# A convolution and low-rank mixer kernel: the batch quarters load in another order, the last quarter of batch 2 waits behind a GpSimd copy and a convolution, and one table is made by a multiplication

## The chip, the cores and the metric

The kernel runs on one core of a Trainium2 chip. The metric is the device time of one execution in microseconds (us); shorter is better. Engines are called PE (TensorE matmul), PEld (its weight load), DVE (VectorE), ACT (ScalarE), POOL (GpSimd) and SP (SyncE); L12 is line 12 of the kernel.

## The reference

The input `x` has 8 batches of 4224 rows by 192 columns. First comes a causal convolution of 7 taps along the rows, with one softmaxed set of weights for each of 8 groups of 24 columns. Then comes a mixer: a low-rank product along the rows, a residual, and a two-layer network along the columns.

```python
w = np.exp(weight - weight.max(-1)); w = w / (w.sum(-1) + 1e-9)       # 8 heads, 7 taps
x_unf = x_pad[:, idx, :].reshape(B, S, K, H, group)
y = np.einsum('hk,bskhg->bshg', w, x_unf).reshape(B, S, D)             # the convolution
h = y.transpose(0, 2, 1) @ U @ V                                       # rank 32, along the rows
u = y + h.transpose(0, 2, 1)
out = u + np.maximum(u @ w_ch1, 0.0) @ w_ch2                           # 192 -> 768 -> 192
```

## The kernel before, in words

All 8 x 33 = 264 tiles of 128 rows are numbered in one row and cut into 33 groups of 8 tiles. A group `g` goes through these steps: `h_group(g)` (L499) multiplies the low-rank factor by `V` on PE (L467) and DVE adds the convolution's result (L490), which gives `u_sb`; `transp(g)` (L507) has SP issue a DMA transpose of `u_sb` into `uT` (L509); `w1(g)` (L573) is the first layer on PE (36 matmuls, L585), whose results ACT (L599) and DVE (L601) take through the ReLU into `rl_sb`; `w2(g)` (L606) is the second layer (L612), DVE adds the residual (L621), and SP issues the store (L629). The stores and the transposes stand in one queue, SP's, in program order. PSUM has 8 banks, which all matmul results use in turn (`bank()`, L56).

A batch `b` is loaded by `x_part` (L76, L79) in four DMAs, cast from float32 to bfloat16, that POOL issues. The tile `x_sb` has two halves of 64 partitions (`r` = 0 and 1), and each half is cut in two along the columns of blocks; the list `XP` (L84) gives the order of these quarters. Two `x_sb` buffers serve in turn, and `x_load` (L639) holds a quarter back until a given matmul is done (`held`, L631).

Batches 0 and 1 are convolved by `conv` (L363), which needs the loaded tile alone. Batches from 2 on use `conv32` (L329), which also needs a copy `xb_sb`, shifted by one block of rows. `x_shift` (L294) makes it in six steps on POOL: `same(s0, s1)` (L301) copies all 128 partitions of some blocks, and `ahead(r, s0, s1)` (L313) overwrites a quarter of the partitions of one half. There is one `xb_sb` buffer.

The order of everything is written by hand in `SLOTS` (L648): each slot names the groups for `w1`, the groups for `w2`, and the jobs that stand between the quarters of `w2`. `do` (L785) carries out a job: "h4" is `h_group(4)` with its transpose, "l2:3" loads quarter 3 of batch 2, "d1" is the convolution of batch 1 by `conv`, followed by `transp(3)`, which is held until the last matmul of that convolution; "x2:6" runs six steps of `x_shift(2)`; "c2:0:3:AAD" is a part of `conv32` for batch 2; "t1" and "s1" are the low-rank sum of batch 1. From batch 3 on, the quarters are loaded from inside `w1` (`LOADS`, L699), and with each load one of the remaining `x_shift` steps is issued.

At the head, `rq` (L153 to L156) is a table of 128 rows by 2 columns: 32 and -128 times the row's quarter number. L178 and L229 read it on the way to the convolution's bands.

Of the kernel before, what the change touches and what calls it, by code (L numbers as in the profile page):

```python
# [7 lines left out]
ALU = mybir.AluOpType  # L8
# [6 lines left out]
def kernel(  # L15
# [10 lines left out]
    nc = tc.nc  # L26
# [14 lines left out]
    QB = 32  # L41
# [14 lines left out]
    def bank():  # L56
        return psp.tile([P, 512], F32, name="ps", tag="ps")
# [9 lines left out]
    NB0 = 32  # L67
    NB1 = S // HB - NB0
# [4 lines left out]
    def x_zero(b, eng):  # L73
        eng.memzero(xt[b][0:HB, 0, :])

    def x_part(b, r, s0, s1):  # L76

        blk = NB0 * r + s0 - 1
        return nc.gpsimd.dma_start(  # L79
            out=xt[b][HB * r : HB * r + HB, s0:s1, :],  # L80
            in_=x[b, blk * HB : (blk + s1 - s0) * HB, :].rearrange("(j p) d -> p j d", p=HB),
        )

    XP = [(0, 1, 17), (0, 17, NB0 + 1), (1, 0, 18), (1, 18, NB1 + 1)]  # L84

    KP = [{0: (0, 10), 1: (0, 10)}, {1: (10, NB1 // 2)}, {0: (10, NB0 // 2)}]

# [15 lines left out]
    def iota(t, pattern, base, mul):  # L103
# [20 lines left out]
        out=Ur[:, 0:nfull, :], in_=U4[0 : nfull * P, :].rearrange("(k p) c -> p k c", p=P)  # L124
# [10 lines left out]
    for q in range(4):  # L135
        src = moe_V[:, 0 : full * 8 * P].rearrange("r (k q t) -> r k q t", q=4, t=2 * P)
        nc.gpsimd.dma_start(
            out=V_sb[32 * q : 32 * q + 32, 0 : 2 * full, :].rearrange(
                "r (k a) t -> r k (a t)", a=2
            ),  # L140
# [3 lines left out]
    for hf in range(2):  # L144
        nc.gpsimd.dma_start(
            out=W1_sb[HB * hf : HB * hf + HB, :, :],
# [5 lines left out]

    rq = cst.tile([P, 2], F32, name="rq")  # L153
    for r in range(4):
        for n, v in enumerate((32.0, -128.0)):
            nc.vector.memset(rq[QB * r : QB * r + QB, n : n + 1], v * r)  # L156
    wps = bank()

    def idle(n, w=4):
# [15 lines left out]
    for hh in range(2):  # L175
# [3 lines left out]
        out=dif[:], in0=dif[:], scalar1=rq[:, 0:1], scalar2=None, op0=ALU.add  # L179
# [5 lines left out]
        out=d_sb[:],  # L185
        in0=w_sb[:],
# [7 lines left out]
        out=hot[:],  # L194
        in0=dif[:].unsqueeze(1).to_broadcast([P, KC, BW]),
# [5 lines left out]
        out=ident[:], in0=fp[:], scalar1=float(P), scalar2=None, op0=ALU.is_equal  # L201
# [9 lines left out]
        out=c_sb[:].rearrange("p k h -> p h k"),  # L211
        in0=e_sb[:],
# [4 lines left out]
    for hh in range(2):  # L217
# [3 lines left out]
            out=pr[:],  # L221
            in0=hot[:].unsqueeze(2).to_broadcast([P, KC, HQ, BW]),
# [7 lines left out]
        out=Eq[:], in0=efp[:], scalar1=rq[:, 1:2], scalar2=None, op0=ALU.is_equal  # L230
# [3 lines left out]
        out=fp[:], in0=fp[:], scalar1=R - 1, scalar2=None, op0=ALU.bitwise_and  # L234
# [3 lines left out]
        out=R4[:], in0=fp[:], scalar1=0.0, scalar2=None, op0=ALU.is_equal  # L238
# [55 lines left out]
    def x_shift(b):  # L294


        xbt[b] = xbs.tile([P, NB1, D], BF16, name="xb_sb")

        def same(s0, s1, *rest):
            def step():  # L300
                nc.gpsimd.tensor_copy(out=xbt[b][:, s0:s1, :], in_=xt[b][:, s0 + 1 : s1 + 1, :])  # L301
                for t0, t1 in rest:
                    nc.gpsimd.tensor_copy(
                        out=xbt[b][HB : HB + QB, t0:t1, :],
                        in_=xt[b][HB : HB + QB, t0 + 1 : t1 + 1, :],
                    )

            return step

        def ahead(r, s0, s1):  # L310
            def step():
                q = slice(HB * r + QB, HB * r + HB)
                nc.gpsimd.tensor_copy(out=xbt[b][q, s0:s1, :], in_=xt[b][q, s0:s1, :])  # L313

            return step

        m = NB0 // 2
        return [
            same(0, m),
            same(m, NB0, (NB0, NB1)),  # L320
            ahead(0, 0, m),
            ahead(0, m, NB0),
            ahead(1, 0, m),
            ahead(1, m, NB1),
        ]

    steps = []

    def conv32(b, h0, nh, engs):  # L329


        if yt[b] is None:
            yt[b] = ys.tile([P, NT, D], BF16, name="y_sb")
        nk = (NB0 // 2, NB1 // 2)
        for n in range(nh):
            h = h0 + n
            hs = slice(h * GS, h * GS + GS)
            pp = [bank(), bank()]
            for cg in range(4):
                t, w, st = (  # L340
                    (xt[b], bands[h // HQ][:, h % HQ, QB : 2 * QB], 1 + cg // 2)
                    if cg % 2
                    else (xbt[b], band2[:, h, :], cg // 2)
                )
                for r in range(2):
                    hr = slice(HB * r, HB * r + HB)
                    nc.tensor.matmul(  # L347
                        out=pp[r][QB * cg : QB * cg + QB, 0 : nk[r] * GS],
                        lhsT=w[hr],
                        rhs=t[hr, st : st + 2 * nk[r] - 1 : 2, hs],  # L350
                        start=True,
                        stop=True,
                        tile_position=(HB * r, QB * cg),
                    )
            for part in range(2):
                j0 = NB0 // 2 * part
                evac(
                    engs[(2 * n + part) % len(engs)],
                    yt[b][:, j0 : j0 + nk[part], hs],
                    pp[part][:, 0 : nk[part] * GS].rearrange("p (k a) -> p k a", a=GS),  # L360
                )
# [58 lines left out]
    def tt_split(b, p):  # L420

        hi = sml.tile([P, D], BF16, name="tt_hi")
        lo = sml.tile([P, D], BF16, name="tt_lo")
        nc.scalar.activation(out=hi[:], in_=p[:, 0:D], func=ACT.Copy)  # L424
        nc.vector.tensor_tensor(out=lo[:], in0=p[:, 0:D], in1=hi[:], op=ALU.subtract)
        ttb[b] += [hi, lo]
# [6 lines left out]
    def tt_sum(b):  # L433
        p = bank()
        for n, part in enumerate(ttb[b]):
            nc.tensor.matmul(  # L436
                out=p[:, 0:D],
                lhsT=R4[:],
                rhs=part[:],
                start=(n == 0),  # L440
                stop=(n + 1 == len(ttb[b])),
            )
        tt_done(b, p)
# [10 lines left out]
    done = []  # L454
# [44 lines left out]
    def h_group(g):  # L499
        t0, t1 = g * GT, g * GT + GT  # L500
        while t0 < t1:
            b = t0 // NT
            te = min(t1, (b + 1) * NT)
            h_tiles(b, t0 - b * NT, te - b * NT)
            t0 = te

    def transp(g):  # L507
        uTt[g] = uts.tile([P, 4, 3, P], BF16, name="uT")
        return nc.sync.dma_start_transpose(  # L509
            out=uTt[g][:].rearrange("p i c t -> p (i c) t"),  # L510
            in_=ut[g][:].rearrange("p i c f k -> p (i c f k)"),
        )
# [118 lines left out]
    def held(ins, after):  # L631
        tc.add_manual_dep(
            ins.ins,
            after.ins.name,
            mybir.DependencyInfo(mybir.DependencyClass.Sync, mybir.DependencyReason.DATA),
            reason="transfer held back",
        )

    def x_load(b, q, after):  # L639
        if q == 0:  # L640
            x_tile(b)
            x_zero(b, nc.gpsimd)
        held(x_part(b, *XP[q]), after)

# [2 lines left out]

    SLOTS = [  # L648
        ([0], [], {}),
        ([1], [0], {0: ["h0", "l2:0", "l2:1"], 1: ["h3", "l2:2"], 2: ["l2:3"]}),  # L650
        ([2], [1], {0: ["d1", "h1"], 1: ["t1"], 3: ["s1"], 4: ["h4", "x2:6"]}),
        ([3], [2], {1: ["h5"], 3: ["h6"]}),
        (
            [4, 5],
# [14 lines left out]
    for k in range(5, 14):  # L669
# [13 lines left out]
        elif k < 10:  # L683
            b = k - 2
# [40 lines left out]
    x_zero(1, nc.gpsimd)  # L725
    x_part(1, *XP[0])
    o = 0
    for r, (k0, k1) in KP[2].items():
        j = NB0 // 2 * r + k0
        nc.gpsimd.tensor_copy(  # L730
            out=U4_sb[:, o : o + k1 - k0, :, :],
# [9 lines left out]
        out=V_sb[0:32, 2 * (NT // 8), :], in_=moe_V[:, (NT - 1) * P : NT * P]  # L741
# [32 lines left out]
    band2 = cst.tile([P, H, QB], BF16, name="band2")  # L774
    for xp in XP[1:]:
        x_part(1, *xp)
    for r in range(4):
        q = slice(QB * r, QB * r + QB)
        for hh in range(2):
            nc.gpsimd.tensor_copy(  # L780
                out=band2[q, HQ * hh : HQ * hh + HQ, :],
# [3 lines left out]
    def do(what):  # L785
        if what[0] == "c":
            b, h0, n, engs = what[1:].split(":")
            conv32(int(b), int(h0), int(n), engs)
            return
        if what[0] == "d":  # L790
            for h in range(H):
                last = conv(int(what[1:]), h, 1, [0, 1], "AA" if h == 2 else "AD")
            held(transp(3), last)
            return
        if what[0] == "l":
            b, q = (int(v) for v in what[1:].split(":"))
            x_load(b, q, done[-1])
            return
        if what[0] == "x":
            b, n = (int(v) for v in what[1:].split(":"))  # L800
            steps.extend(x_shift(b))
            for _ in range(n):
                steps.pop(0)()
            return
        n = int(what[1:])
        if what[0] == "h":
            h_group(n)
            if n > 1 and n != 3:
                transp(n)
        elif what[0] == "t":  # L810
            tt_split(n, tt_mm(n, range(NT)))
        else:
            tt_sum(n)
# [55 lines left out]
```

## Time and profile before

| | us |
|---|---|
| median of 3 runs (lowest, highest) | 325.52 (325.27, 325.65) |
| the profiled execution's own time | 325.04 |
| span of the profiled execution | 323.3 |
| PE busy in the span | 316.1 (98%) |
| DVE busy | 268.7 (83%) |
| ACT busy | 169.6 (52%) |
| POOL busy | 141.1 (44%) |

The span is counted from the first instruction to the last end; 325.04 - 323.3 = 1.7 us lie around it. A matmul's end is modelled in the profile, so that a busy PE is not PE at its peak. In the views a wait is written "who waited <- what released it".

### The profile page before, as it was taken

What the parts mean: (1) busy time and instruction counts of PE and PEld (TensorE: products, weight loads), DVE (VectorE), ACT (ScalarE), POOL (GpSimd) and SP (SyncE); (2) the same over time, 40 slices, a digit from 0 to 9 for tenths busy, and PEclk for the clock granted to TensorE, in tenths of its full rate; (3) what the DMA queues carried; (4) which work ended last, traced back from release to release, by engine and by line L of the source; (5) the groups of instructions that cost most, each with busy time, mean ns of one, the idle gap of its engine ahead of it and who ended that gap; (6) DMA issues with size and microseconds to landing.
All of it is one profiled execution on the core that took longest, in us unless ns stands there. A gap on an engine that the chain in (4) does not pass through costs nothing.

```text
span 323.3 us, 9598 instructions
## 1 busy us (share of the span) xinstructions
PE 316.1 (98%) x4004; PEld 223.7 (69%) x4004; DVE 268.7 (83%) x553; ACT 169.6 (52%) x344; POOL 141.1 (44%) x108
## 2 busy tenths in 40 slices
PE   7999999999999999999999999999999999999994
PEld 3757577578678648877864884696796497497494
DVE  6779989987977986997898699789888888896853
ACT  1766723960973496098249509915804903903900
POOL 8764069828947984991986596000000000000000
PEclk9999999999999999999999999999999999999999
DMA  9999994999999999899589965148098089059044
GB/s 105 192 194 171 193 237 102 189 172 273 210 123 199 255 140 193 155 178 214 163 213 183 209 162 159 52 132 241 23 190 250 3 165 276 2 143 248 2 133 162
DMA packets 122443, 53.39 MB, mean 165 GB/s; under 512 B 87712, under 2 KB 122400, under 8 KB 122400
## 3 DMA queue, kind: packets, MB, share of 16 engines
q1 hardware_dynamic: 84528, 38.08, 47.4%
q0 software_dynamic: 37728, 14.60, 39.2%
q8 instruction: 31, 0.51, 0.6%
q14 instruction: 12, 0.10, 0.1%
q10 hardware_dynamic: 144, 0.10, 0.1%
HBM read 29.22 MB, written 25.95 MB: 171 GB/s over the span
## 4 chain that ended last, share of the span: by engine, by line
PE 90%; ACT 4%; DMA 2%; DVE 2%; issue 1%; POOL 0%; POOLq 0%
PE ps L612 42%; PE ps L585 39%; PE ps L347 3%; PE ps L467 3%; DMA x_sb<-in_x_dram 2%; PE ps L410 2%; ACT rl_sb L599 2%; ACT y_sb L264 2%; PE ps L377 1%; DVE u_sb L490 1%; DVE rl_sb L601 1%; PE ps L436 0%; PE ps L532 0%; POOL x_sb L79 0%; DVE out_sb L621 0%
## 5 line engine op out<-in xcount | busy, mean ns | idle before, releaser
L599 ACT ACTIVATE rl_sb<-ps 128x512 bf16<-128x512 f32 x233 | 124.3, 604 | 107.7 <-PE ps L585 100.1
L612 PE MATMUL ps<-W_sb,rl_sb 128*128 128x192 bf16 x1584 | 141.2, 246 | 0.2
L612 PEld LDWEIGHTS <-rl_sb 128*128 128x128 bf16 x1584 | 128.3, 98 | 11.8 <-issue 11.4
L585 PE MATMUL ps<-uT,W_sb 64*128 64x512 bf16 x1188 | 131.5, 376 | 0.4 <-DVE uT L266 0.2
L601 DVE TENSOR_SCALAR rl_sb<-ps 128x512 bf16<-128x512 f32 x163 | 105.2, 686 | 15.0 <-PE ps L585 14.7
L585 PEld LDWEIGHTS <-W_sb 64*128 64x128 bf16 x1188 | 67.2, 94 | 60.2 <-issue 3.6
L621 DVE TENSOR_TENSOR out_sb<-ps,u_sb 128x384 f32<-128x384 f32 (+1 forms) x133 | 70.2, 548 | 25.5 <-PE ps L612 25.1
L313 POOL COPY xb_sb<-x_sb 32x3072 bf16<-32x3072 bf16 (+1 forms) x24 | 67.4, 2824 | 0.5
L490 DVE TENSOR_TENSOR u_sb<-y_sb,ps 128x192 bf16<-128x192 bf16 (+1 forms) x168 | 66.2, 458 | 0.0
L301 POOL COPY xb_sb<-x_sb 128x3072 bf16<-128x3072 bf16 x12 | 32.6, 2742 | 43.0 <-PE ps L347 31.3
L264 ACT ACTIVATE y_sb<-ps 128x384 bf16<-128x384 f32 (+4 forms) x90 | 38.3, 520 | 9.7 <-PE ps L347 7.4
L79 POOL DMA_DIRECT2D x_sb<-in_x_dram x32 | 27.1, 853 | 11.4 <-PE ps L467 7.7
L266 DVE CAST y_sb<-ps 128x408 bf16<-128x408 f32 (+4 forms) x36 | 19.1, 577 | 1.3 <-PE ps L377 1.2
L467 PE MATMUL ps<-tt_sb,V_sb 32*128 32x192 bf16 x264 | 12.4, 246 | 0.1
L347 PE MATMUL ps<-xb_sb,band 64*32 64x384 bf16 x192 | 12.1, 332 | 0.0
L347 PE MATMUL ps<-x_sb,band 64*32 64x384 bf16 x192 | 12.1, 333 | 0.0
L467 PEld LDWEIGHTS <-V_sb 32*128 32x128 bf16 x264 | 4.7, 92 | 7.3 <-issue 7.3
L424 ACT ACTIVATE tt_hi<-ps 128x192 bf16<-128x192 f32 x8 | 2.6, 330 | 11.9 <-PE ps L410 11.9
L377 PE MATMUL ps<-x_sb,band 64*64 64x240 bf16 (+3 forms) x192 | 7.9, 276 | 0.4 <-DMA x_sb<-in_x_dram 0.3
L347 PEld LDWEIGHTS <-band 64*32 64x32 bf16 x384 | 4.6, 89 | 5.2 <-issue 2.4
L377 PEld LDWEIGHTS <-band 64*64 64x64 bf16 x192 | 6.0, 106 | 2.2 <-issue 1.5
L161 PE MATMUL ps<-zz 128*128 128x512 f32 (+1 forms) x10 | 6.4, 785 | 1.1 <-DVE zz L151 1.1
(64 smaller groups left out, 68.0 us busy)
## 6 DMA issues: line engine op xcount, KB each, us to landing
out_dram<-out_sb SPq DMA_DIRECT2D x131, 192.0 KB, 2.9
x_sb<-in_x_dram POOLq DMA_DIRECT2D x14, 384.0 KB, 7.4
x_sb<-in_x_dram POOLq DMA_DIRECT2D x7, 432.0 KB, 7.6
x_sb<-in_x_dram POOLq DMA_DIRECT2D x7, 408.0 KB, 8.9
W_sb<-in_moe_w_ch_dram POOLq DMA_DIRECT2D x3, 288.0 KB, 7.6
x_sb<-in_x_dram POOLq DMA_DIRECT2D x1, 504.0 KB, 7.4
uT<-u_sb SPq DMA_TRANSPOSE x31, 3.7
x_sb<-in_x_dram POOLq DMA_DIRECT2D x1, 480.0 KB, 5.7
```

The costliest lines, as they stand in the source:

```text
L79: return nc.gpsimd.dma_start(out=xt[b][HB * r : HB * r + HB, s0:s1, :], in_=x[b, blk * HB : (blk + s1 - s0) * HB, :].rearrange("(j p) d -> ...
L264: nc.scalar.activation(out=out, in_=in_, func=ACT.Copy)
L301: nc.gpsimd.tensor_copy(out=xbt[b][:, s0:s1, :], in_=xt[b][:, s0 + 1 : s1 + 1, :])
L313: nc.gpsimd.tensor_copy(out=xbt[b][q, s0:s1, :], in_=xt[b][q, s0:s1, :])
L347: nc.tensor.matmul(out=pp[r][QB * cg : QB * cg + QB, 0 : nk[r] * GS], lhsT=w[hr], rhs=t[hr, st : st + 2 * nk[r] - 1 : 2, hs], start=True, ...
L467: last = nc.tensor.matmul(out=banks[pr][:, a * D : (a + 1) * D], lhsT=V_sb[32 * q : 32 * q + 32, (j // 8) * 2 + j % 2, :], rhs=ttb[b][32 * ...
L490: nc.vector.tensor_tensor(out=u_group(g)[:, i : i + n, :, hf, :], in0=yt[b][:, run[0] : run[0] + n, :].rearrange("p n (c k) -> p n c k", c=3),
L585: last = nc.tensor.matmul(out=pps[m][hf][:], lhsT=W1_sb[HB * hf : HB * hf + HB, c, m * P : (m + 1) * P], rhs=uTt[g][HB * hf : HB * hf + HB ...
L599: nc.scalar.activation(out=rl[:, m, hf, :], in_=pp[hf][:], func=ACT.Relu)
L601: nc.vector.tensor_scalar_max(out=rl[:, m, hf, :], in0=pp[hf][:], scalar1=0.0)
L612: last = nc.tensor.matmul(out=cps[:, a * D : (a + 1) * D], lhsT=rlt[g][:, m, hf, (i + a) * P : (i + a + 1) * P], rhs=W2_sb[:, m, :], start ...
L621: nc.vector.tensor_tensor(out=o[:, 0:n, :].rearrange("p n (c k) -> p n c k", c=3), in0=cps[:, 0 : n * D].rearrange("p (n c k) -> p n c k", ...
```

## The change

Three things are changed. The table `rq` is made by four fills of its first column and one DVE multiplication by -4 for the second, instead of eight fills. The list `XP` now has the first quarters of both halves ahead of the second ones; the steps of `x_shift` are put in the matching order, so that the first three steps need the first two quarters alone. And the last quarter of batch 2, which was loaded in slot 2 of the list (groups 1 and 0), goes one slot later: it is issued after the convolution of batch 1 and after the first step of `x_shift(2)` in POOL's program, and is held until the last matmul of that convolution; the other five steps follow it.

```diff
-    XP = [(0, 1, 17), (0, 17, NB0 + 1), (1, 0, 18), (1, 18, NB1 + 1)]
+    XP = [(0, 1, 17), (1, 0, 18), (0, 17, NB0 + 1), (1, 18, NB1 + 1)]
 ...
     rq = cst.tile([P, 2], F32, name="rq")
     for r in range(4):
-        for n, v in enumerate((32.0, -128.0)):
-            nc.vector.memset(rq[QB * r : QB * r + QB, n : n + 1], v * r)
+        nc.vector.memset(rq[QB * r : QB * r + QB, 0:1], float(QB * r))
+    nc.vector.tensor_scalar(
+        out=rq[:, 1:2], in0=rq[:, 0:1], scalar1=-4.0, scalar2=None, op0=ALU.mult
+    )
 ...
             same(0, m),
+            ahead(0, 0, m),
+            ahead(1, 0, m),
             same(m, NB0, (NB0, NB1)),
-            ahead(0, 0, m),
             ahead(0, m, NB0),
-            ahead(1, 0, m),
             ahead(1, m, NB1),
 ...
-        ([1], [0], {0: ["h0", "l2:0", "l2:1"], 1: ["h3", "l2:2"], 2: ["l2:3"]}),
-        ([2], [1], {0: ["d1", "h1"], 1: ["t1"], 3: ["s1"], 4: ["h4", "x2:6"]}),
+        ([1], [0], {0: ["h0", "l2:0", "l2:1"], 1: ["h3", "l2:2"]}),
+        (
+            [2],
+            [1],
+            {0: ["d1", "x2:1", "l2:3", "x2:5", "h1"], 1: ["t1"], 3: ["s1"], 4: ["h4"]},
+        ),
 ...
             held(transp(3), last)
+            done.append(last)
             return
 ...
             b, n = (int(v) for v in what[1:].split(":"))
-            steps.extend(x_shift(b))
+            if not steps:
+                steps.extend(x_shift(b))
```

## The prediction

> **What bounds the kernel now.** I read the page's busy times and its chain first.
>
> ```profile
> PE 316.1 (98%) x4004; PEld 223.7 (69%) x4004; DVE 268.7 (83%) x553; ACT 169.6 (52%) x344; POOL 141.1 (44%) x108
> PE 90%; ACT 4%; DMA 2%; DVE 2%; issue 1%; POOL 0%; POOLq 0%
> ```
>
> PE is busy for 98% of the span and makes 90% of the chain that ended last. POOL, the engine whose order the change rewrites, has no share of it. From 80.5 us on the chain is PE alone, in pieces of constant length (108 matmuls of L585 in 11.76 us, 48 of L612 in 4.07 us), so nothing that the change moves can shorten or lengthen that part unless it makes PE wait. What can move is the head and the stretch from 28 to 82 us. The view of waits for that stretch has only these rows in which PE stands behind something that the change touches, or behind its neighbour:
>
> ```profile
> POOL xb_sb L301 <- DMA x_sb<-in_x_dram: 11.7, 2, 10.5
> ...
> PEld L585 <- DMA uT<-u_sb: 0.3, 1, 0.3
> PEld L585 <- DVE u_sb L490: 0.3, 1, 0.3
> ```
>
> The first is POOL's own (10.47 us for batch 2, 1.22 for batch 3); the second is PE waiting for the transpose of group 3, which "d1" holds back; the third follows 1.5 us later, for a PSUM bank. The timeline of POOL, and then of SP, places them:
>
> ```profile
> 29.03 3.36 POOL L79 DMA_DIRECT2D x_sb<-in_x_dram  x4 [7.69 <-PE ps L467]
> 42.87 5.43 POOL L301 COPY xb_sb<-x_sb 128x3072 bf16<-128x3072 bf16 x2 [10.47 <-DMA x_sb<-in_x_dram]
> 48.35 0.50 POOL L303 COPY xb_sb<-x_sb 32x384 bf16<-32x384 bf16 x1
> 48.90 11.24 POOL L313 COPY xb_sb<-x_sb 32x3072 bf16<-32x3072 bf16 x4
> 60.20 0.17 POOL L74 MEMSET x_sb<- 64x96 uint32 x1
> ```
>
> ```profile
> 40.41 1.43 SPq L509 DMA_TRANSPOSE uT<-u_sb  x1
> ```
>
> ```profile
> 46.25 0.56 DVE L621 TENSOR_TENSOR out_sb<-ps,u_sb 128x384 f32<-128x384 f32 x1 [0.33 <-PE ps L612]
> 46.66 0.33 PEld L585 LDWEIGHTS <-W_sb 64*128 64x128 bf16 x6 [0.33 <-DMA uT<-u_sb]
> ```
>
> The four quarters of batch 2 are issued at 29.03, 29.87, 30.71 and 31.55 (3.36 / 4 = 0.84 each); the DMA view, asked window by window, gives 5.9, 8.1, 12.1 and 13.8 us to landing: 34.9, 38.0, 42.8 and 45.4. The transpose issued at 40.41 takes 6.2 us to landing, 46.6, and PE starts w1(3) at 46.66, 0.33 late. The transposes issued at 48.81 and 54.63, with no load in flight, take 3.2.
>
> **The change, part by part.** The sum is made against the profiled execution, 325.04 us (span 323.3); the median of the runs is 0.48 above it, and I carry the difference over to the median.
>
> *The table rq.* Eight fills take 0.40 us from 0.95, 0.05 each. Four go (-0.20), and a multiplication over 128x1 comes; the nearest row is L206, 128x8 in 0.17, and small dependent DVE operations start 0.20 to 0.29 apart (L204 at 5.06, L206 at 5.30, L208 at 5.50, L210 at 5.74). So the column is ready about 0.1 us earlier to 0.2 later.
>
> ```profile
> 0.95 0.40 DVE L156 MEMSET rq<- 32x1 f32 x8
> ...
> 3.54 0.85 DVE L178 TENSOR_SCALAR dif<-dif,rq 128x38 f32<-128x38 f32 x1 [1.42 <-POOL dif L104]
> ```
>
> Behind it DVE has only the zeroing of the bands and of a strip of x_sb, done at 2.11, and then stands 1.42 us until POOL's iota: that is the cover, so the cost is 0. Without the cover it would be 0.2 us at most. One row warns: L178 takes 0.85 us for 38 elements where L200 takes 0.30 for 128, and it ends at 4.39, just after POOL's iota for efp (3.72 + 0.62 = 4.34). A small DVE operation can thus be kept until a POOL instruction ends, and the new multiplication falls beside POOL's first two DMA issues (1.25 to 3.21). Kept till 3.21, the zeroing (0.55 + 0.14) would end near 3.9 to 4.1: still before 4.34, so 0. The other way round, POOL's first issue kept back by a multiplication of up to 0.2 us moves the load that starts PE (landed 9.67): up to +0.2. I take 0.
>
> The Trainium skill, page "SBUF — State Buffer", section "SBUF: two separate sides", says that a VectorE operation in a two-port mode and a GpSimd operation exclude each other for the whole instruction; it also says that GpSimd cannot write DMA descriptors meanwhile. By it the multiplication speaks against the change, with the two outcomes just priced; without it the sum is the same 0.
>
> *The order of the quarters.* Batch 1's convolution (at 37.1) needs all four quarters from its first head on; the last is issued near 18.0 and takes 12.5 us, landing near 30.6. Reordering three of them costs 0, with 6 us of cover. From batch 3 on, POOL's steps add up to the same work in the same slots; batch 3 loses its 1.22 us wait, because the fourth step, not the second, needs the last quarter. The steps of batch 3 end at 91.25, PE asks for them at 94.4; those of batch 4 end at 118.06, PE asks at 120.6. All of it lies beside PE: 0.
>
> *The last quarter of batch 2.* POOL's queue becomes: three issues from 29.03 to 31.55; the first copy, which needs the first two quarters; the issue of the last quarter; the other five steps. The second issue now carries 432 KB instead of 384, so it should land near 38.5 (38.0 plus 48 KB at the 90 KB/us at which the third, 432 KB, followed it: 4.8 us). The copy takes 2.74, to 41.25. The convolution ends on PE at 40.29, so the copy, not the hold, sets the issue: 41.25 to 42.1. The first load's packets appear in the trace about 2 us after its issue, so the quarter moves from about 43.3 and lands at 47 to 50 (5.9 us as the first quarter, 8.2 as the median load between 10 and 95 us). Queued behind this waiting POOL are two copies of 2.74 (to 47.6), then the big copy (to 50.4 or 52.8), 0.50, 2.74 and 3.08: POOL is free at 57 to 59 instead of 60.2. PE asks for xb_sb of batch 2 only at 66.2. Then the loads of batch 3, today kept at POOL until 60.2, start 1 to 3 us earlier; their readers are 91 us away. On the path: 0.
>
> *The transpose of group 3.* In the trace's packet records the stores and transposes share one queue. Today the transpose's packets start at 43.0 and crawl at about 270 a us while loads run, then finish 1000 in one us once the loads stop at 44.4. After the change the loads pause from about 41.5 to 43.3, so the transpose (1536 packets) should land at 44 to 45.5. The 0.33 us wait goes. What is late next is DVE: it drains the banks of "h4" in order from 46.72 on, and the third pair of banks of w1(3) is free only at 48.11, where PE waits 0.26 now. DVE's chain starts from the matmuls before w1(3), not from the transpose; started 0.33 earlier, PE would wait up to 0.59 there. So the gain is between 0 and 0.33; the DVE row is the nearer one, and I take 0.1.
>
> *Stores and the next transposes.* The last quarter now runs beside the stores of w2(1) and perhaps the transpose of group 4 (issued 48.81, landing 52.0, needed at 55.7: 3.7 us of cover). DMA engines are nearly idle from 48 to 56 (0.41 of 6 us), so the backlog is worked off there: 0.
>
> *POOL beside DVE.* The first copy moves under the eviction of batch 1's convolution (38 to 41.3). Seven casts of 128x408 take 3.51 us there with POOL idle. L490 x6 takes 2.06 us beside POOL's copies (52.50) and 2.07 with POOL idle (64.58): no effect, 0; if it did slow DVE and ACT there by a tenth, it would be 0.3 us.
>
> Sum: 0 + 0 + 0 - 0.1 + 0 = -0.1: a profiled 324.9, a median of 325.4.
>
> **The rivals.** About 0.2%, 0.65 us, is what a measurement of this kernel can tell from no change.
>
> *Faster.* The wait for uT may be longer in ordinary executions than in the profiled one, which is faster than all three timed runs. If the whole 0.48 us to the median is this wait, the change can take away 0.33 + 0.48 = 0.81: 324.7. Against it stands the DVE row, which gives part of it back, and that the trace shows one execution only.
>
> *Slower.* The last quarter starts into the transpose instead of after it. The transpose issued at 66.67 amid the loads of batch 3 took 8.9 us. With that, uT of group 3 lands at 40.41 + 8.9 = 49.3 instead of 46.6; less the 0.26 of slack at the banks, that is +2.4: 327.9. At 7.6 us, the middle of 6.2 and 8.9, it is +1.1: 326.6. It decides from a landing of 46.9 on. For it: both would be issued within 2 us of each other. Against it: one quarter of 408 KB at some 150 KB/us lasts under 3 us, and today the transpose already runs beside as much.
>
> *Nothing to hold.* If the copy ends before the convolution, the hold at 40.29 sets the issue, the quarter starts near 42.3 and the transpose lands near 46, as today: 325.5.
>
> **How the numbers follow.** Forecast and "nothing to hold" together 0.67, all within 0.2%; faster 0.18; slower 0.13; the head late by 0.2 us, also within, 0.02. The range reaches from just past the faster rival's 324.7 to near the slower rival's half-way price: 324.5 to 326.3.
>
> **What would show it.** Right: POOL's first copy of batch 2 starts near 38.5, the last quarter is issued near 41.3, POOL's steps end by 59, the wait of L585 for uT is gone, the wait for DVE's u_sb has grown toward 0.6, and w2(2) starts at 50.7 to 50.8 as before; at the head L178 still ends at 4.4 and the first convolution starts at 9.7. Wrong: uT of group 3 landing after 46.9, a PE wait for xb_sb, the first load issued later than 1.25, or longer pieces of PE after 80 us.

## The result: faster by 1.25 us, and the profile shows the gain behind the last matmul

Over 12 executions of each, the changed kernel takes a median of 324.37 us (324.11 to 325.25), the kernel before 325.62; the ratio is 0.9963 with a 95% interval of 0.9948 to 0.9978. The profiled execution took 324.34 us with a span of 322.4, against 325.04 and 323.3. The lowest times differ by 1.02 us and the two spans by 0.87; the rest of the 1.25 lies in how far the executions of a kernel spread. The ratios, here and below, leave out executions more than 1.5% above the fastest of their kernel (one each of "before, 24 fills", "changed, 4 fills" and "before, 8 bytes"), the medians keep them.

The page of the changed kernel, its busy times and its chain, in the form shown before:

```profile
PE 316.4 (98%) x4004; PEld 223.3 (69%) x4004; DVE 268.9 (83%) x550; ACT 169.6 (53%) x344; POOL 141.8 (44%) x108
PE 91%; ACT 4%; DMA 2%; DVE 2%; issue 1%; POOL 0%; POOLq 0%
```

Nothing on PE became shorter. DVE has three instructions fewer here (550 for 553; the fourth that is gone is a semaphore operation, which the page does not count). In the middle the profile shows what was forecast. First the waits between 28 and 82 us (waited for, us in total, times, longest), then POOL's and SP's timeline and the start of w1(3):

```profile
POOL xb_sb L303 <- DMA x_sb<-in_x_dram: 6.7, 1, 6.7
...
PEld L587 <- DVE u_sb L492: 0.4, 1, 0.4
```

```profile
38.34 2.74 POOL L303 COPY xb_sb<-x_sb 128x3072 bf16<-128x3072 bf16 x1 [6.72 <-DMA x_sb<-in_x_dram]
41.02 0.88 POOL L79 DMA_DIRECT2D x_sb<-in_x_dram  x1
41.95 5.52 POOL L315 COPY xb_sb<-x_sb 32x3072 bf16<-32x3072 bf16 x2
...
56.81 0.17 POOL L74 MEMSET x_sb<- 64x96 uint32 x1
```

```profile
40.51 1.40 SPq L511 DMA_TRANSPOSE uT<-u_sb  x1
```

```profile
46.35 0.56 DVE L623 TENSOR_TENSOR out_sb<-ps,u_sb 128x384 f32<-128x384 f32 x1 [0.33 <-PE ps L614]
46.59 0.33 PEld L587 LDWEIGHTS <-W_sb 64*128 64x128 bf16 x6 [0.16 <-issue]
```

PE's wait for uT is gone; the wait for a bank that DVE drains has grown from 0.26 to 0.43 us instead. Matched one by one, the matmuls of the two executions stand 0.10 us later at 45 us and 0.10 us later at 137, 229 and 283 us. The 0.10 us is there from the first convolution on, where PE waits 0.44 us for its load instead of 0.34; it is not the table's, for with the table alone (below) the matmuls stand 0.05 us earlier there. The last matmul ends at 319.21 us, against 319.11 before. The kernel whose PE ends 0.10 us later has a span that is 0.87 us shorter: in these two executions the whole gain lies behind the last matmul. I call what lies between its end and the end of the span the tail: 323.27 - 319.11 = 4.16 us before, 322.40 - 319.21 = 3.19 after.

The DMA view of the tail, from 319 to 322.3 us, shows why. Before (the first line gives GB/s in 40 slices of 0.08 us; then queue, packets, MB, share of 16 engines; then issues with KB and median us to landing):

```profile
GB/s 382 363 177 19 0 0 0 56 270 434 354 344 354 344 308 363 326 363 345 372 298 103 9 9 28 19 28 19 28 19 28 19 28 0 0 0 0 0 0 0
...
q14 instruction: 1, 0.01, 1.4%
...
out_dram<-out_sb SPq DMA_DIRECT2D x1, 192.0 KB, 2.9
out_dram<-out_sb SPq DMA_DIRECT2D x1, 96.0 KB, 2.7
out_dram<-out_sb ACTq DMA_DIRECT2D x1, 96.0 KB, 2.6
```

The same view after:

```profile
GB/s 372 372 372 242 47 0 0 0 19 223 372 363 382 363 382 345 363 372 354 382 372 326 140 9 0 0 0 0 0 0 0 0 0 0 0 0 0 0 0 0
...
out_dram<-out_sb SPq DMA_DIRECT2D x1, 192.0 KB, 1.9
out_dram<-out_sb SPq DMA_DIRECT2D x1, 96.0 KB, 1.7
out_dram<-out_sb ACTq DMA_DIRECT2D x1, 96.0 KB, 1.7
```

Before, the three last stores land 0.9 to 1.0 us later, after a trickle of 19 to 28 GB/s, packets of 768 B one behind the other, 33 ns apart: one DMA engine of the 16, still at work when the others are done. In the same window stands one packet of the kind "instruction" on queue 14: 8 KB, from 319.8 us on, 0.75 us long. After, the window has no such packet. Between 319.85 and 320.05 us the packet records have 15 store packets and the instruction packet in flight, 16 in all, as many as there are DMA engines: it takes the place of one engine's stores. The records do not name the engine of a packet; that the engine that is late is this one is inferred from the count.

Why it was there is a matter of counting. The trace holds 707 DVE instructions before (semaphore operations and drains included) and 703 after. Before, the 576th starts at 261.13 and an 8 KB packet follows at 261.33; the 704th, 128 further on, is the DRAIN behind the last residual addition, at 319.15, and the packet follows at 319.82. After, the 576th starts at 262.95 with a packet at 263.00, and a 704th does not exist. 8 KB over 128 instructions is 64 B for each. The Trainium skill, page "Runtime: NRT & Kernel Launch", section "Instruction fetch mechanics", says that each sequencer fetches its next instructions over a DMA queue of its own in blocks of 16 KiB, and calls the cost mostly hidden; the blocks of queue 14 are 8 KB here. A block that comes 7 us before the end leaves the end where it is ("before, 14 pieces" below), one among the last stores does not.

### The profile page after: what moved, and what is told of

The parts are those of the page before. It is cut to its first block, busy times and chain, and to the rows that moved or that the text cites. A ratio compares the mean times of both kernels' runs of the same rounds, so it can differ in the third digit from the quotient of the medians.

```text
span 322.4 us, 9590 instructions
## 1 busy us (share of the span) xinstructions
PE 316.4 (98%) x4004; PEld 223.3 (69%) x4004; DVE 268.9 (83%) x550; ACT 169.6 (53%) x344; POOL 141.8 (44%) x108
## 4 chain that ended last, share of the span: by engine, by line
PE 91%; ACT 4%; DMA 2%; DVE 2%; issue 1%; POOL 0%; POOLq 0%
PE ps L614 42%; PE ps L587 39%; PE ps L349 3%; PE ps L469 3%; DMA x_sb<-in_x_dram 2%; PE ps L412 2%; ACT rl_sb L601 2%; ACT y_sb L266 2%; PE ps L379 1%; DVE u_sb L492 1%; DVE rl_sb L603 1%; PE ps L438 0%; PE ps L534 0%; POOL x_sb L79 0%; DVE out_sb L623 0%
```

## Experiments

Theory T says that the tail is decided by whether DVE's 704th instruction falls among the last stores. Rival O says that the gain comes from the order of the transfers. First, the two halves of the change by themselves, and T's cause added without either of them, or with both.

**Table alone** (the kernel before, with rq by four fills and a multiplication).

> Edit: the kernel before with the new making of rq alone (four fills and a multiplication); quarters and batch 2 as before. Theory T (the tail): DVE's instructions become 703 instead of 707, its DRAIN after the last residual addition is no longer its 704th, and the 8 KB instruction fetch that stood at 319.8 us among the last stores falls away; the last store lands about 0.9 us earlier, span near 322.4, ratio to before near 0.996 to 0.997, although PE's last matmul is no earlier. Rival O (the order): the gain comes from the transfers of batch 2 and the earlier transpose of group 3; this kernel has none of it and stays at the time of before, ratio 0.999 to 1.001, span near 323.3.

**Order alone** (the changed kernel, with rq by eight fills).

> Edit: the changed kernel with rq made by eight fills as before; the order of quarters and the last quarter of batch 2 as changed. Theory T: DVE's count is about 707 again, the fetch stands among the last stores, time as before, ratio 0.999 to 1.001; the transpose of group 3 lands near 45.2 as in the changed kernel, PE waits longer for u_sb in its place. Rival O: the gain stays, ratio near 0.996.

**The kernel before with 24 fills more**

```diff
+    spare = cst.tile([P, 2], F32, name="spare")
+    for _ in range(24):
+        nc.vector.memset(spare[:], 0.0)
```

> Edit: the kernel before plus 24 DVE fills of a spare tile at the head, where DVE stands idle 1.4 us; more work, nothing else moved. Theory T: DVE's 704th instruction comes 24 instructions earlier, near 306 us, the fetch with it; the delayed stores are caught up long before the end and the tail is short: span 322.4 to 322.6, ratio 0.996 to 0.998, faster by doing more. Rival O, and any theory in which less DVE work is what helps: ratio 1.000 or above.

**The changed kernel with 4 fills more** (the same lines with `range(4)`).

> Edit: the changed kernel plus 4 DVE fills of a spare tile at the head (0.2 us of DVE time in its idle 1.4 us). Theory T: DVE's count is 707, its DRAIN is the 704th again, the fetch returns near 319.9 and the last store lands about 0.9 us later: span near 323.3, ratio to before 0.999 to 1.001. Rival O: the gain of the changed kernel stays, ratio near 0.996.

**The changed kernel, zeroing in pieces, 4 instructions more**

```diff
-    for hh in range(2):
-        nc.vector.memzero(bands[hh][:])
+    for q in range(4):
+        nc.vector.memzero(bands[0][:, q, :])
+    for q in range(2):
+        nc.vector.memzero(bands[1][:, 2 * q : 2 * q + 2, :])
```

> Edit: the changed kernel, with the zeroing of the two bands at the head cut in 4 and 2 pieces: 4 more DVE instructions for the same bytes, no new tile and no new wait (the fills of a spare tile waited for one another and moved every later tile by 8 bytes). Theory T (the place of the instruction fetch): DVE counts 707, its DRAIN is the 704th, the 8 KB fetch returns at 319.9; from PE's last matmul to the end of the span 4.2 us instead of 3.3, lowest time 325.0 to 325.3 where the changed kernel has 324.1. Rival O (the order of transfers): 3.3 us and a lowest time of 324.1 to 324.4.

**The kernel before, zeroing in 16 pieces, 14 instructions more**

```diff
-        nc.vector.memzero(bands[hh][:])
+        for q in range(HQ):
+            for c in range(2):
+                nc.vector.memzero(bands[hh][:, q, HB * c : HB * c + HB])
```

> Edit: the kernel before, with the zeroing of the bands cut in 16 pieces: 14 more DVE instructions for the same bytes, no new wait. Theory T: DVE's 704th instruction is now a residual addition or its semaphore 14 places earlier, near 314 us; the fetch comes while 5 or 6 more stores follow, and the delay is caught up: tail 3.3 us, lowest time 324.2 to 324.5, with the table and the order of before. Rival O: tail as before or time as before, lowest near 325.2.

**The kernel before, moved by 8 bytes** (the spare tile without a fill).

> Edit: the kernel before, with an unused tile of 8 bytes a partition behind rq, which moves every later tile of its pool by 8 bytes, as in the two runs with fills of a spare tile. If the shift is what spread those runs (5 us and more between their lowest and highest), this one spreads as they did, median 326.5 or more with the same tail of 4.2 us. If not, it is before over again: ratio 0.998 to 1.002.

**The changed kernel again**

> The changed kernel once more, on the chip of the other three. Theory T and rival O alike: ratio near 0.9963, lowest 324.1 to 324.4, tail 3.3 us. It is there so that the pieces and the shift are compared with it on one chip.

**The changed kernel, 3 instructions more** (band 0 zeroed in 4 pieces, band 1 in one).

> Edit: the changed kernel, with the zeroing of the first band in 4 pieces: 3 more DVE instructions, 706 in all, one fewer than in the run with 4 more. Theory T: the DRAIN behind the last addition is DVE's 703rd, the 704th is a semaphore operation that waits until all stores have landed; the fetch comes too late to meet a store: tail 3.2 us, lowest 324.1 to 324.4, ratio 0.996 to 0.998. A theory in which a few more DVE instructions lengthen the tail by degrees: tail between 3.2 and 4.1, near 3.9.

What was measured, in one table. "Tail" is from the end of PE's last matmul to the end of the span in the profiled execution, "fetch" the start of the packet of queue 14 beside DVE's 704th instruction, where there is one. The ratio is to the kernel before on the same chip, with its 95% interval; the lowest time of the kernel before was 325.13, 325.19 (table alone to 4 fills), 324.91 (4 pieces to changed again) and 324.83 (3 pieces), its median 325.62, 326.15, 325.34 and 325.46.

| kernel | DVE instr. | fetch at | last matmul ends | tail | lowest | median | ratio |
|---|---|---|---|---|---|---|---|
| before | 707 | 319.8 | 319.11 | 4.16 | 325.13 | 325.62 | 1 |
| changed | 703 | none | 319.21 | 3.19 | 324.11 | 324.37 | 0.9963 (0.9948 to 0.9978) |
| table alone | 703 | none | 319.38 | 3.19 | 324.35 | 324.66 | 0.9959 (0.9940 to 0.9978) |
| order alone | 707 | 319.9 | 319.13 | 4.14 | 325.08 | 325.62 | 0.9977 (0.9954 to 1.0000) |
| before, 24 fills | 730 | 314.4 | 324.12 | 3.34 | 324.62 | 326.56 | 1.0007 (0.9977 to 1.0036) |
| changed, 4 fills | 707 | 324.1 | 323.36 | 4.26 | 325.20 | 327.30 | 1.0033 (0.9999 to 1.0066) |
| changed, 4 pieces | 707 | 321.1 | 320.42 | 4.11 | 324.95 | 325.77 | 1.0003 (0.9987 to 1.0018) |
| before, 14 pieces | 721 | 313.4 | 319.15 | 3.21 | 324.10 | 324.37 | 0.9966 (0.9950 to 0.9981) |
| before, 8 bytes | 707 | 321.1 | 320.40 | 4.10 | 325.03 | 325.97 | 1.0016 (0.9994 to 1.0038) |
| changed again | 703 | none | 320.54 | 3.20 | 324.26 | 324.57 | 0.9965 (0.9949 to 0.9980) |
| changed, 3 pieces | 706 | 321.2 | 319.08 | 3.20 | 323.98 | 324.50 | 0.9976 (0.9953 to 0.9999) |

The tails fall into two groups, 4.10 to 4.26 where there are 707 DVE instructions and 3.19 to 3.34 where there are not. The table alone has the whole gain. The order alone has the lowest time and the tail of before, and its matmuls stand within 0.03 us of before; PE's wait for uT is gone there too, though the transpose took 5.6 us to landing, about 46.0 and not the 45.2 that was expected. Its ratio, 0.9977, lies under T's 0.999 to 1.001, with an interval that ends at 1.0000. "Before, 14 pieces" has the old table and the old order, does the same zeroing in more instructions, and gains as much as the change: the work was not what cost time. Its fetch falls at 313.4 us, amid stores too, but the last store ends only 7 us later, at 320.9. "Changed, 4 pieces" has the new table and the new order and no gain. Between 706 and 707 instructions, one instruction more is 0.9 us: with 706 the fetch starts at 321.2, after the last store's end at 320.8. The DMA view of the tail with 4 pieces (319.6 to 323.6 us), and then with 3 (318.3 to 322.2):

```profile
GB/s 8 0 0 61 307 369 384 369 353 123 0 0 0 92 300 451 346 353 338 323 369 331 331 384 192 23 23 23 23 23 23 23 23 23 0 0 0 0 0 0
...
q14 instruction: 1, 0.01, 1.2%
...
out_dram<-out_sb SPq DMA_DIRECT2D x1, 96.0 KB, 2.7
out_dram<-out_sb ACTq DMA_DIRECT2D x1, 96.0 KB, 2.6
```

```profile
GB/s 0 0 0 150 347 370 378 378 315 79 0 0 0 118 354 362 378 370 370 355 362 355 363 378 237 32 0 0 0 84 0 0 0 0 0 0 0 0 0 0
...
q14 instruction: 1, 0.01, 0.5%
...
out_dram<-out_sb SPq DMA_DIRECT2D x1, 96.0 KB, 1.7
out_dram<-out_sb ACTq DMA_DIRECT2D x1, 96.0 KB, 1.7
```

With 4 pieces one engine's trickle of 23 GB/s is back; with 3 the lone 84 is what comes after the stores, where the fetch stands by itself.

**What missed.** The two kernels with fills of a spare tile have the tails that T gives, but not the times: their medians were to be faster by 0.2 to 0.4% and the same as before, and they are 1.0007 and 1.0033, with PE's last matmul 4 to 5 us late in the profile. The fetch with 24 fills came at 314.4, not near 306. Part of the lateness lies at the head: the 24 fills took 2.98 us, one after the other, so that the first band came 1.06 us late, and 0.36 of it was left in PE's matmuls at 18 us. The rest comes later, and in other kernels too. In the waits of "changed, 4 fills" between 60 and 110 us:

```profile
DVE out_sb L626 <- DMA out_dram<-out_sb: 3.6, 1, 3.6
```

and in its chain between 66 and 100 us (start, us, what):

```profile
69.89 9.95 DMA out_dram<-out_sb
```

DVE waits for the store of an earlier out_sb to land, and cannot write the next: eight buffers are full, because nine stores stand in SP's queue behind the transpose of group 7 (issued at 66.67, 11.3 us to landing), which itself runs beside the loads of batch 3. "Changed again" shows it with 1.5 us and a last matmul 1.3 us late, "changed, 4 pieces" with 1.4. It strikes some executions and kernels of both kinds. In "before, 24 fills" the wait is 1.2 us and PE loses 0.84 us around it; the larger losses there, 1.75 us near 154 and 2.04 near 177 (where PE waits 1.7 us for POOL's xb_sb), lie elsewhere, and what starts them stays open. Whether the 8 bytes by which the spare tile moves the others add to it stayed open: "before, 8 bytes" gives 1.0016, with an interval over 1, and one execution of 332.09. Its late matmuls (by 0.8 us near 154 and 0.2 near 177) have other places.

**Twelve buffers for out_sb**, on the changed kernel: `name="outs", bufs=8` becomes `bufs=12`.

> Edit: the changed kernel with 12 buffers for out_sb instead of 8. In some profiled executions of kernels of both kinds DVE waits 1.2 to 3.6 us near 80 us for a store to land before it can write the next out_sb, with the stores queued behind the transpose of group 7 and the loads of batch 3; PE then comes out 1 to 4 us late. Theory W: that wait is what spreads the executions; with 12 buffers it is gone from the profile, PE's last matmul is within 0.3 us of 319.2, the times gather at 324.1 to 324.6, and the version is the fastest of all by the median, by 0.1 to 0.3 us, with the same lowest time. Rival: the wait is only one sign of crowded transfers, and PE is late by the transpose instead; the spread stays, with highest times over 325.5.

It takes 324.15 us (324.03 to 324.23 over 8 executions), ratio 0.9946 (0.9925 to 0.9966), while "changed, 3 pieces" on the same chip ran from 323.98 to 326.57. The spread has gone from 2.6 us to 0.2, with the same lowest time. No late execution of "changed, 3 pieces" was profiled; that this wait made its spread is taken from the other kernels. The transpose of group 7 still took 9.4 us; only nobody waits for the stores behind it. This is the fastest version of all by the median. (It has 720 DVE instructions, its last fetch at 314.5 and a tail of 3.19, so T has its part in it.)

## Why the prediction failed, step by step

*The forecast* was 325.4 with a range from 324.5 to 326.3, and "within 0.2%" as the likeliest; measured were 324.37 us and a gain of 0.37%.

*The step that failed* is in the first paragraph: "nothing that the change moves can shorten or lengthen that part unless it makes PE wait". The sum ended with PE's last matmul, and the 4.16 us behind it were taken to stay. They were 0.97 us shorter. The chain that was read for this stops at DVE's last addition, at 319.51 us (319.15 + 0.36), 3.76 us before the end of the span; its last pieces before the change:

```profile
315.97 3.15 PE ps L612 x38
319.12 0.02 issue
319.15 0.36 DVE out_sb L621
```

The DMA view had a sign of it: the last stores took 2.6 to 2.9 us to landing, as long as the median of the 131 stores of 192 KB (2.9) amid other traffic, but at the end nothing else was in flight except an instruction packet at 319.8.

*The table rq* was costed in time alone: "0", and so it is. Four fills took 0.37 us where eight had taken 0.40, and not the half; with the multiplication, 0.15 us from 1.36, the column was ready at 1.51 instead of 1.35, within the forecast. The zeroing began 0.05 later, and DVE's wait for the iota was 1.39 instead of 1.42:

```profile
0.96 0.37 DVE L155 MEMSET rq<- 32x1 f32 x4
1.36 0.15 DVE L156 TENSOR_SCALAR rq<-rq 128x1 f32<-128x1 f32 x1
...
3.55 0.85 DVE L180 TENSOR_SCALAR dif<-dif,rq 128x38 f32<-128x38 f32 x1 [1.39 <-POOL dif L104]
```

POOL's first two issues took the same 1.96 us beside it, and the multiplication was not held until they ended, so the exclusion that I weighed from the Trainium skill ("SBUF — State Buffer", "SBUF: two separate sides") did not show at this place; whether the multiplication ran in a two-port mode, no run shows. The row that warned has its like in "before, 24 fills": there the 0.85 us operation starts at 4.96, after POOL's last iota has ended (3.74 + 0.62 = 4.36), and takes 0.25. That fits an operation that is kept beside the iotas. What the part on the table missed is that four instructions fewer move every later fetch of DVE's program.

*The last quarter of batch 2* went as worked out: the first copy at 38.34 (forecast 38.5), the issue at 41.02 (41.25), landing at 47.2 (47 to 50), POOL free at 56.8 (57 to 59). Only the first three loads of batch 3 became earlier; the last is held by PE and was issued at 63.69, as before at 63.59. None of it is on the path, as said.

*The stores and the next transposes.* The 0.41 was misread: it is not a time but the share that the DMA engines were busy from 50 to 56 us, so they were not nearly idle. Nothing followed from it: the transpose of group 4 took 3.2 us to landing as before.

*The transpose of group 3* landed at 40.51 + 4.7 = 45.2 (44 to 45.5), and DVE's bank took the wait over, as said. I took 0.1 us of gain between 0 and 0.33; it was 0, the end that the DVE row spoke for.

*The rival "faster"* had the sign and the wrong mechanism. It laid the 0.48 us between the profiled execution and the median on the wait for uT. The order alone gives 0.9977 (0.9954 to 1.0000), and with the new table but 707 instructions 1.0003 (0.9987 to 1.0018): a share of the order of some tenths of a per cent is not excluded by the first and not seen in the second.

*The rivals "slower" and "nothing to hold"* did not come about: the last quarter's packets began at 44, when the transpose's were nearly through.

## What to carry to other kernels

Read the tail of a profile by itself: when the last matmul ends, how long the last stores take to land, and what else is in flight then. An edit's cost is not only its time; the number of instructions on an engine shifts where its program is fetched, and here a fetch among the last stores cost 0.9 us that a few instructions more or fewer took away, so a gain of that size should be tested with a dummy instruction before it is credited to the edit. And where the times of one kernel spread while its lowest time stays, look for a buffer that is reused just after a slow transfer.

## What the runs showed of the hardware

An 8 KB instruction packet took 0.67 to 0.75 us among the last stores and held back the stores on one of the 16 DMA engines, and with it the end, by 0.9 us. In all twelve traces a packet of queue 14 starts within 1.1 us of DVE's 576th recorded instruction and, where there is one, within 0.8 us of its 704th, semaphore operations and drains counted; at the 64th, 192nd, 320th and 448th the distance is up to 9.4 us. The records do not name the engine whose program a packet of queue 14 carries: that it is DVE's is inferred from these places and from the step between 706 and 707. A DMA transpose beside four loads took 8.7 to 11.3 us to landing, where it took 3.2 alone.
